# Graph aggregation with a sorted edge list: one allowance per tile for the second part's work, and evictions on VectorE after it

## The chip, the cores and the metric

The kernel runs on one core of a Trainium2 chip. The metric is the device time of one execution in microseconds (us). A core has engines that run side by side, each in its own order and waiting for the others by semaphores: TensorE (PE; its weight loads are PEld), VectorE (DVE), ScalarE (ACT), GpSimd (POOL) and SyncE (SP, which only issues DMAs here).

## What is computed

12,500 nodes have 64 features each; 800,000 edges have a source and a destination. For every node the features of its edges' sources are summed, scaled by a given number per node, and two 64 x 64 products are added:

```python
def reference(x, src, dst, deg_inv, w_self, w_neigh):
    N = x.shape[0]
    nsum = _segment_sum(x[src], dst, N)
    h_neigh = nsum * deg_inv[:, None]
    return x @ w_self + h_neigh @ w_neigh
```

The edges are random, so nothing is known of their order.

## The kernel before

Each edge becomes a 32-bit key: which block of 160 destinations and which block of 128 sources it joins (98 x 78 = 7644 such pairs, called buckets), and the places in both blocks. 128 partitions sort 6250 keys each; then the sorted runs are brought together. This is done in two parts: part 0 holds the first 4736 buckets, part 1 the rest. For each part, windows of the sorted runs are gathered by GpSimd to one row per partition (`gather_runs`), the row is merged (`merge_runs`, mostly minima and maxima on VectorE, L416 and L456), each bucket's start is searched (`find_and_gather`: a count, L616, on VectorE for part 1, then a gather, L620, on GpSimd), and the buckets are decoded (`decode_buckets`: `split` on VectorE, L657 to L662, `narrow` and `turn`, L667 to L678, casts on ScalarE and transposes on TensorE). A bucket has 128 slots; what doesn't fit is kept by its eight largest of each piece (`pieces`, L711) and put in order by `leftovers`. `tail` does the last few nodes, which no block of 160 holds. `check` sums counters to see that every edge is found.

The sums are the loop `nodes`: 962 tiles of eight buckets. VectorE makes two one-hots for 28 buckets at a time (`ohs` L838, `ohd` L841, together called a pair here), as far as 44 buckets ahead. TensorE multiplies one with the source features into a tile `ct` in PSUM (L867); an engine evicts it to `xg` (ScalarE L877, or VectorE L875); TensorE multiplies `xg` with the other one-hot into an accumulator (L923) that holds six blocks of destinations, 73.5 tiles. Leftover edges come in as gathered rows `lx` (GpSimd L887, five held at a time) with a mask `ohl` (VectorE L895) and two matmuls (L903). `finish` multiplies the sums by the weights and writes the output.

The order is the code's own here: every engine runs its instructions in the order in which the program writes them. While `nodes` goes on with part 0's buckets, the rest of part 1's work is written between its tiles, by `sums_and_merge`. There, n is the tile. From tile 8 on, PACE = 420 is added to t for each tile, and merge steps are written while t is above zero; each gives its cost in ns, which is taken off t. They stop after the first stages until tile 100 (RESUME). After the merge the search goes a step every second tile, then the decoding a step every tile, and then the leftovers; t plays no part in these. From tile 503 on (SHARE) every second tile is evicted by VectorE if enough one-hots are ready; the check is written at once behind the leftovers.

Of the kernel before, what the change touches and what calls it, by code (L numbers as in the profile page):

```python
# [11 lines left out]
F32 = mybir.dt.float32  # L12
# [21 lines left out]
KPRS = (37, 23)  # L34
# [24 lines left out]
PACE = 420  # L59
SHARE = 503  # L60
# [87 lines left out]
def on_act2(part, k):  # L148

    return part == 0 and (k < NLOWER or (k - NLOWER) % 2 == 0)  # L150
# [111 lines left out]
class Kernel:  # L262
# [381 lines left out]
    def decode_buckets(self, part, v, vp, mps):  # L644
# [51 lines left out]
        nc.vector.tensor_tensor(e, ext, bases(0, kpr, EXT), op=OP.bitwise_xor)  # L696
        f = e.bitcast(F32)
# [8 lines left out]
        yield kpr  # L706

    def pieces(self, f, n, top, pcs):

        for j in range(pcs):  # L710
            self.nc.vector.max(out=top[:, j, :8], in_=view(f, j, [[pcs, len(range(j, n, pcs))]]))  # L711

    def leftovers(self, part, mps):
# [6 lines left out]
        self.pieces(self.top.rearrange("p j i -> p (j i)"), PCS * 9, top.bitcast(F32), REST)  # L720
        k = top.rearrange("p j i -> p (j i)")
        yield 1
# [8 lines left out]
        yield 1  # L731
# [4 lines left out]
        nc.vector.scalar_tensor_tensor(q, t, float(HN), q, op0=OP.mult, op1=OP.add)  # L736
        nc.vector.tensor_scalar(t, k, 14, 1, op0=OP.logical_shift_right, op1=OP.bitwise_and)
# [3 lines left out]
        yield 1  # L741
# [18 lines left out]
    def tail(self, mps):  # L760
# [7 lines left out]
        yield  # L768
        yield
# [74 lines left out]
    def nodes(self, pool, aps, mps):  # L844
# [151 lines left out]
    def check(self, pool, mps):  # L996

        nc = self.nc
        self.flag = self.keep.tile([1, 1], I32, name="flag")
        ones = pool.tile([128, 1], F32, name="ones")  # L1000
        nc.vector.memset(ones, 1.0)
        one = pool.tile([128, 1], F32, name="one")
        nc.vector.tensor_reduce(one, self.cnt, axis=mybir.AxisListType.X, op=OP.add)
        ps = mps.tile([1, 1], F32, name="fps", tag="ct", bufs=3)
        nc.tensor.matmul(ps, one, ones, start=True, stop=True)
        nc.vector.tensor_scalar(self.flag, ps, float(E), None, op0=OP.not_equal)
# [119 lines left out]
    def sums_and_merge(self, es, mps, aps, u1, other, l2, l2b, l2a, va, vp):  # L1126
# [32 lines left out]
        self.picked, self.used = -9, 0  # L1159
        left, left_at = self.leftovers(0, mps), 2  # L1160
        t = 0
        for n in self.nodes(fin, aps, mps):
            if left and n >= left_at:
                wait = next(left, None)
                if wait is None:
                    left = None
                    if 1 in self.left:
                        self.check(fin, mps)
                else:
                    left_at = n + wait  # L1170
            if runs and n % 3 == 0:
                self.gather_runs(1, u1, [runs.pop(0)])
            if tail and n % 2:
                next(tail, None)
            if merge and n >= 8 and (n >= RESUME or steps < 2 * per):
                t += PACE
                while merge and t > 0:
                    dt = next(merge, None)
                    steps += 1
                    if dt is None:  # L1180
                        merge = None
                        self.merged = True
                        assert self.rows is u1
                        l2b.close()
                        vp = vb.enter_context(tc.tile_pool(name="vb", bufs=1))
                        self.windows(1, vp)
                        self.store_rows(2, tc.nc.scalar)
                        find = self.find_and_gather(1, range(KPRS[1]), LAG)
                    else:
                        t -= dt  # L1190
            elif find:
                if n % 2 == 0 and self.picked < n - 1 and next(find, None) is None:
                    find = None
                    decode = self.decode_buckets(1, self.v, vp, mps)
                    tail = self.tail(mps)
            elif decode:
                if next(decode, None) is None:
                    assert n < 128 * KPRS[0] // 8 - 12
                    decode = None
                    left, left_at = self.leftovers(1, mps), 0  # L1200
        vb.close()
# [28 lines left out]
```

## Time and profile before

| what | us |
|---|---|
| median of 3 runs | 1882.71 (1881.04 to 1889.39) |
| profiled execution | 1888.32 |
| its span, first to last instruction | 1886.6 |
| VectorE busy | 1667.2 |
| ScalarE busy | 1169.7 |
| TensorE busy with matmuls | 980.7 |
| GpSimd busy | 809.9 |

Busy times overlap, so they don't add up. A row of a table by stretches gives the stretch and its length, then for each engine its busy time and, in brackets, the number of instructions, then the granted TensorE clock as a share, the DMA's share and GB/s. A row of the timeline gives start, length, engine, line, operation, what is written and read, a count, and in square brackets how long the engine was idle before and what ended it. A row of waits gives who waited for whom: total, times, longest. A group's row gives the count, busy time, mean in ns, and idle time before with what ended most of it.

### The profile page before, as it was taken

The numbers are of one execution on the slowest core, as the hardware profiler recorded it, in microseconds if no ns is written. First come the engines' busy times: TensorE is split into PE (matmuls) and PEld (weight loads), VectorE is DVE, ScalarE is ACT, GpSimd is POOL, SyncE is SP. The second block draws the span as 40 slices with busy tenths as digits, with TensorE's granted clock in tenths as the row PEclk, the third lists the DMA queues.
The fourth block names the chain that finished last, engine by engine and source line by source line (L and its number), as shares of the span: only waits on it lengthen the run. The fifth ranks groups of instructions, "written<-read, shape, count | busy, mean of one in ns | idle before, by whom it ended". The sixth has DMA issues, their size and how long they took to land.

```text
span 1886.6 us, 54681 instructions
## 1 busy us (share of the span) xinstructions
PE 980.7 (52%) x23698; PEld 839.0 (44%) x23698; DVE 1667.2 (88%) x1805; ACT 1169.7 (62%) x1868; POOL 809.9 (43%) x917
## 2 busy tenths in 40 slices
PE   0015100000000000185888888888868989988997
PEld 0003100000000000174777777777757778777886
DVE  6999999999559999797799999998897888888885
ACT  7435128206500032485898888889977877877786
POOL 1000000798889986888713131313552142222321
PEclk9998655555555555598899999999999999999999
DMA  4304100011100012476678877779766888788784
GB/s 153 70 0 100 36 32 7 21 35 38 22 19 9 10 45 79 127 267 194 211 228 240 264 238 262 244 253 329 264 203 228 267 274 264 253 277 254 247 261 144
DMA packets 104805, 305.25 MB, mean 162 GB/s; under 512 B 52945, under 2 KB 60491, under 8 KB 103915
## 3 DMA queue, kind: packets, MB, share of 16 engines
q1 hardware_dynamic: 86347, 277.44, 41.7%
q0 software_dynamic: 17632, 22.17, 8.8%
q8 instruction: 187, 3.06, 0.6%
q10 hardware_dynamic: 576, 2.07, 0.3%
q14 instruction: 63, 0.52, 0.1%
HBM read 282.20 MB, written 19.41 MB: 160 GB/s over the span
## 4 chain that ended last, share of the span: by engine, by line
DVE 42%; PE 25%; POOL 13%; issue 10%; ACT 5%; DMA 4%; DVEq 0%; SPq 0%; ACTq 0%; POOLq 0%
DVE u L456 15%; PE ct L867 13%; POOL u L394 10%; PE acc L923 9%; DVE b L230 6%; DVE a L230 6%; DVE ohd L841 6%; DVE ohs L838 4%; DMA slb<-sl 2%; ACT xg L877 2%; POOL pad L307 2%; POOL lx L887 1%; DVE u L416 1%; PE acc L903 1%; POOL v L620 1%
## 5 line engine op out<-in xcount | busy, mean ns | idle before, releaser
L877 ACT ACTIVATE xg<-ct 128x1024 f16<-128x1024 f32 (+1 forms) x898 | 852.2, 1033 | 187.3 <-PE ct L867 154.8
L867 PE MATMUL ct<-xh,ohs 128*128 128x128 f16 x7644 | 545.4, 224 | 80.3 <-DVE ohs L838 40.0
L867 PEld LDWEIGHTS <-ohs 128*128 128x128 f16 x7644 | 450.2, 100 | 125.6 <-issue 64.2
L394 POOL DMA_INDIRECT u<-d,ix x256 | 374.0, 1461 | 178.8 <-DVE ix L386 135.4
L923 PE MATMUL acc<-ohd,xg 64*128 64x80 f16 x15288 | 405.9, 199 | 64.2 <-issue 48.9
L456 DVE TENSOR_TENSOR u<-u 128x1456 f32<-128x1456 f32 (+51 forms) x314 | 398.1, 1291 | 19.7 <-ACT u L421 13.6
L923 PEld LDWEIGHTS <-xg 64*128 64x128 f16 x15288 | 319.7, 96 | 135.0 <-issue 65.2
L841 DVE TENSOR_TENSOR ohd<-iota,dlT 128x2240 f16<-128x2240 bf16 x273 | 359.8, 1318 | 0.0
L838 DVE TENSOR_SCALAR ohs<-slb,pidx 128x3584 f16<-128x3584 bf16 x273 | 314.7, 1153 | 35.1 <-PE ct L867 16.6
L887 POOL DMA_INDIRECT lx<-xt,lsrc x140 | 231.2, 1652 | 261.6 <-PE acc L903 228.4
L230 DVE TENSOR_TENSOR b<-a 128x608 f32<-128x608 f32 (+44 forms) x124 | 173.8, 1444 | 6.3 <-ACT a L232 2.3
L230 DVE TENSOR_TENSOR a<-b 128x608 f32<-128x608 f32 (+44 forms) x124 | 173.9, 1445 | 4.5
L994 POOL DMA_DIRECT2D out<-o x25 | 23.7, 949 | 339.6 <-DVE o L993 257.6
L384 PE MATMUL stp<-idf,st 128*128 128x128 f32 x2 | 0.9, 445 | 310.7 <-DVE st L382 310.7
L677 PE MATMUL tr<-idb,l 128*128 128x128 bf16 x60 | 8.0, 273 | 263.9 <-ACT l L671 253.2
L384 PEld LDWEIGHTS stp<-idf,st 128*128 128x128 f32 x2 | 0.4, 183 | 311.1 <-issue 311.1
L875 DVE CAST xg<-ct 128x1024 f16<-128x1024 f32 x64 | 78.2, 1223 | 68.3 <-PE ct L867 63.5
L677 PEld LDWEIGHTS <-l 128*128 128x128 bf16 x60 | 4.9, 117 | 267.1 <-ACT l L671 255.7
L421 ACT ACTIVATE u<-u 128x96 f32<-128x96 f32 (+36 forms) x155 | 32.9, 258 | 134.3 <-DVE u L456 71.1
L375 ACT ACTIVATE junka<-b,c 128x132 bf16<-128x132 f32 (+46 forms) x205 | 90.8, 443 | 12.3 <-DVE b L230 5.8
L232 ACT ACTIVATE b<-a 128x1 f32<-128x1 f32 (+21 forms) x52 | 18.7, 379 | 128.1 <-DVE a L230 122.2
L620 POOL DMA_INDIRECT v<-d,ix x60 | 73.8, 1230 | 55.5 <-ACT ix L638 46.1
(160 smaller groups left out, 795.5 us busy)
## 6 DMA issues: line engine op xcount, KB each, us to landing
slb<-sl SPq DMA_DIRECT2D x273, 896.0 KB
u<-d,ix POOLq DMA_INDIRECT x256
xt<-xh SPq DMA_DIRECT2D x1, 3136.0 KB
fo<-own SPq DMA_DIRECT2D x26, 120.0 KB
own<-os SPq DMA_DIRECT2D x12, 256.0 KB
out<-o POOLq DMA_DIRECT2D x24, 120.0 KB
lx<-xt,lsrc POOLq DMA_INDIRECT x140
rd<-dst SPq DMA_DIRECT2D x4, 521.0 KB
```

What stands on the lines that cost most here:

```text
L230: nc.vector.tensor_tensor(view(dst, lo + sh, [[st, g], [1, l]]), x, y, op=op)
L375: nc.scalar.activation(junks[0][:, :n], w, AF.Sign, bias=self.c1[:, 0, c:c + 1], accum_out=a)
L394: nc.gpsimd.indirect_dma_start(out=u[:nr, EDGE + p * w:EDGE + (p + 1) * w], out_offset=None, in_=src, in_offset=bass.IndirectOffsetOnAxis( ...
L456: nc.vector.tensor_tensor(view(dst, EDGE + o + out, d), view(src, EDGE + o + x, d), view(src, EDGE + o + x + gap, d), op=op)
L620: self.nc.gpsimd.indirect_dma_start(out=self.v[:, k].bitcast(F32), out_offset=None, in_=flat(self.d2[home(part, k)], 128 * PITCH2[home(par ...
L838: nc.vector.tensor_scalar(s.rearrange("p c s -> p (c s)"), b, self.pidx[:, :1], None, op0=OP.is_equal)
L841: nc.vector.tensor_tensor(d, self.iota[:, None].to_broadcast([128, 14, HN, 2]), ix, op=OP.is_equal)
L867: nc.tensor.matmul(ct[:, i * 128:(i + 1) * 128], cols[i][0], self.xh[:, (b0 + i) % NB].rearrange("p a f -> p (a f)"), start=True, stop=True)
L875: nc.vector.tensor_copy(xg[:, :cnt * 128], ct[:, :cnt * 128])
L877: nc.scalar.activation(xg[:, :cnt * 128], ct[:, :cnt * 128], AF.Copy)
L887: nc.gpsimd.indirect_dma_start(out=x, out_offset=None, in_=self.xt, in_offset=bass.IndirectOffsetOnAxis(ap=self.left[p][1][:, c:c + 1], ax ...
L923: nc.tensor.matmul(acc[h][:, db % OCT * HN:(db % OCT + 1) * HN], xg[r, i * 128:(i + 1) * 128], d[r], start=db % OCT == 0 and sb == 0, stop ...
```

## The change

PACE becomes 390 and SHARE goes. t is added to at every tile from the eighth on, except in the pause before tile 100, also when the merge is over: a search step whose count is on VectorE takes 500 off it, and a decoding step is written only if t is above zero, begins five tiles after the search and takes off what it gives: 2300 if it holds a split, 0 if not, 1500, 800, 800, and 900 for each four maxima. So the exclusive or, the two products and the sixteen maxima, which were two steps, become seven. The leftovers of part 1 go a piece every second tile, in one or two pieces more, the tail's first work waits four turns more, and the check is three steps eight tiles apart, after the tail. VectorE evicts a tile only when `spare` is set, which is when part 1's leftovers are done.

```diff
-PACE = 420
-SHARE = 503
+PACE = 390
...
-            yield min(step // 2 * 4, kpr - 1)
+            yield 2300 if step % per == 0 and step // per < len(groups) else 0
...
         nc.vector.tensor_tensor(e, ext, bases(0, kpr, EXT), op=OP.bitwise_xor)
+        yield 1500
...
-        yield kpr
+            yield 800
...
-        self.pieces(f.rearrange("p k h s -> p (k h s)"), kpr * 2 * EXT, top, PCS)
+        for _ in self.pieces(f.rearrange("p k h s -> p (k h s)"), kpr * 2 * EXT, top, PCS, 4):
+            yield 900
...
             self.nc.vector.max(out=top[:, j, :8], in_=view(f, j, [[pcs, len(range(j, n, pcs))]]))
+            if j % per == per - 1:
+                yield
...
-            pend.append(gather(b0, cnt, t >= SHARE))
+            pend.append(gather(b0, cnt, self.spare))
...
         nc.vector.tensor_reduce(one, self.cnt, axis=mybir.AxisListType.X, op=OP.add)
+        yield
         ps = mps.tile([1, 1], F32, name="fps", tag="ct", bufs=3)
         nc.tensor.matmul(ps, one, ones, start=True, stop=True)
+        yield
...
                 if wait is None:
                     left = None
                     if 1 in self.left:
-                        self.check(fin, mps)
+                        self.spare = True
...
-            if tail and n % 2:
-                next(tail, None)
-            if merge and n >= 8 and (n >= RESUME or steps < 2 * per):
-                t += PACE
-                while merge and t > 0:
+            if tail and n % 2 and next(tail, self) is self:
+                tail = None
+            if self.spare and not tail and n % 8 == 0 and verdict != self:
+                verdict = verdict or self.check(fin, mps)
+                if next(verdict, self) is self:
+                    verdict = self
+            if n < 8 or (merge and n < RESUME and steps >= 2 * per):
+                continue
+            t += PACE
+            while merge and t > 0:
...
+            if find and n % 2 == 0 and self.picked < n - 1:
+                k = next(find, None)
+                if k is None:
                     find = None
-                    decode = self.decode_buckets(1, self.v, vp, mps)
                     tail = self.tail(mps)
-            elif decode:
-                if next(decode, None) is None:
+                elif k < KPRS[1] and not on_act2(1, k):
+                    t -= 500
+            if not find:
+                ready += 1
+            if decode and ready > 4 and t > 0:
+                dt = next(decode, None)
+                if dt is None:
...
+                else:
+                    t -= dt
```

Lines from L687 on move by a few (L838 becomes L842, L875 L879, L456 L455). Counted along each engine's order, the merge's end stands behind 410 evictions before and 434 now, the last search step behind 481 and 505, the casts of part 1's buckets between 488 and 510 and between 515 and 538 evictions by ScalarE, and the first eviction by VectorE at about tile 504 and 566; there are 64 of these before and 55 now.

VectorE near the merge's end, before: a merge stage (`u<-u`) stands between any two pairs of one-hots.

```order
L456 TENSOR_TENSOR u<-u 128x1456
L838 TENSOR_SCALAR ohs<-slb,pidx 128x3584
L841 TENSOR_TENSOR ohd<-iota,dlT 128x2240
L456 TENSOR_TENSOR u<-u 128x1456
L838 TENSOR_SCALAR ohs<-slb,pidx 128x3584
L841 TENSOR_TENSOR ohd<-iota,dlT 128x2240
L456 TENSOR_TENSOR u<-u 128x1456
L838 TENSOR_SCALAR ohs<-slb,pidx 128x3584
L841 TENSOR_TENSOR ohd<-iota,dlT 128x2240
```

And now, at the same place:

```order
L455 TENSOR_TENSOR u<-u 128x1456
L842 TENSOR_SCALAR ohs<-slb,pidx 128x3584
L845 TENSOR_TENSOR ohd<-iota,dlT 128x2240
L899 TENSOR_SCALAR ohl<-wide,lp_2834 128x160
L842 TENSOR_SCALAR ohs<-slb,pidx 128x3584
L845 TENSOR_TENSOR ohd<-iota,dlT 128x2240
L455 TENSOR_TENSOR u<-u 128x1456
L842 TENSOR_SCALAR ohs<-slb,pidx 128x3584
L845 TENSOR_TENSOR ohd<-iota,dlT 128x2240
```

Now and then two pairs, 56 buckets, stand between two merge stages.

VectorE where the last buckets of part 1 are decoded, before (`u` is the exclusive or and its products, `top` and `ltop` the maxima, `lz` the start of the leftovers):

```order
L875 CAST xg<-ct 128x1024
L696 TENSOR_TENSOR u<-v,c_1_68 128x1426
L699 SCALAR_TENSOR_TENSOR u<-u,v 128x23x31 x2
L838 TENSOR_SCALAR ohs<-slb,pidx 128x3584
L841 TENSOR_TENSOR ohd<-iota,dlT 128x2240
L703 MEMSET top_18093 128x144
L711 MAX top_18093<-u 128x8 x16
L711 MAX ltop<-top_18093 128x8 x8
L838 TENSOR_SCALAR ohs<-slb,pidx 128x3584
L841 TENSOR_TENSOR ohd<-iota,dlT 128x2240
L725 TENSOR_SCALAR lz,cnt<-ltop 128x64
```

And now:

```order
L695 TENSOR_TENSOR u<-v,c_1_68 128x1426
L699 SCALAR_TENSOR_TENSOR u<-u,v 128x23x31
L842 TENSOR_SCALAR ohs<-slb,pidx 128x3584
L845 TENSOR_TENSOR ohd<-iota,dlT 128x2240
L699 SCALAR_TENSOR_TENSOR u<-u,v 128x23x31
L703 MEMSET top_18968 128x144
L711 MAX top_18968<-u 128x8 x12
L842 TENSOR_SCALAR ohs<-slb,pidx 128x3584
L845 TENSOR_TENSOR ohd<-iota,dlT 128x2240
L711 MAX top_18968<-u 128x8 x4
L711 MAX ltop<-top_18968 128x8 x4
L842 TENSOR_SCALAR ohs<-slb,pidx 128x3584
```

The two products and the maxima have pairs of one-hots between them, and no eviction (`xg<-ct`) stands among them.

GpSimd at the end of the tail's gathers (`tx`), before:

```order
L669 DMA sl<-l_17945 128x384
L788 DMA tx<-xt,ts 128x128
L887 DMA lx<-xt,lsrc_2825 128x128
L788 DMA tx<-xt,ts 128x128 x4
L887 DMA lx<-xt,lsrc_2825 128x128 x2
L994 DMA out<-o 120x4x64
L887 DMA lx<-xt,lsrc_2825 128x128
```

And now:

```order
L668 DMA sl<-l_18726 128x384
L792 DMA tx<-xt,ts 128x128 x2
L891 DMA lx<-xt,lsrc_2836 128x128
L792 DMA tx<-xt,ts 128x128 x5
L998 DMA out<-o 120x4x64
L891 DMA lx<-xt,lsrc_2836 128x128
L792 DMA tx<-xt,ts 128x128
L891 DMA lx<-xt,lsrc_2836 128x128 x4
```

The tail's gathers stand a place later among the leftovers' (`lx`) and the outputs, with at most five of them in a row.

More of the change, by code (lines that the diff above doesn't have):

```diff
@@ L719, in leftovers @@
         top = pool.tile([128, REST, 8], I32, name="ltop")
-        self.pieces(self.top.rearrange("p j i -> p (j i)"), PCS * 9, top.bitcast(F32), REST)
+        for _ in self.pieces(self.top.rearrange("p j i -> p (j i)"), PCS * 9, top.bitcast(F32), REST, 4):
+            yield 1 + part
         k = top.rearrange("p j i -> p (j i)")
-        yield 1
         t = pool.tile([128, n], I32, name="lt")
@@ L730, in leftovers @@
         nc.vector.tensor_tensor(s, s, t, op=OP.bitwise_or)
-        yield 1
+        yield 1 + part
         q = pool.tile([128, n], I32, name="lq")
@@ L736, in leftovers @@
         nc.vector.scalar_tensor_tensor(q, t, float(HN), q, op0=OP.mult, op1=OP.add)
+        if part:
+            yield 2
         nc.vector.tensor_scalar(t, k, 14, 1, op0=OP.logical_shift_right, op1=OP.bitwise_and)
@@ L740, in leftovers @@
         nc.vector.tensor_tensor(z, z, q, op=OP.add)
-        yield 1
+        yield 1 + part
         sel = pool.tile([128, 64], F32, name="sel")
@@ L767, in tail @@
         nc.gpsimd.dma_start(k.bitcast(F32), last.rearrange("(p n) -> p n", n=n))
-        yield
-        yield
+        for _ in range(6):
+            yield
         t = pool.tile([128, n], I32, name="tt")
@@ new lines, in sums_and_merge @@
+            if self.spare and not tail and n % 8 == 0 and verdict != self:
[6 more added lines that the diff above has]
+            while merge and t > 0:
+                dt = next(merge, None)
+                steps += 1
+                if dt is None:
+                    merge = None
+                    self.merged = True
+                    assert self.rows is u1
+                    l2b.close()
+                    vp = vb.enter_context(tc.tile_pool(name="vb", bufs=1))
+                    self.windows(1, vp)
+                    self.store_rows(2, tc.nc.scalar)
+                    find = self.find_and_gather(1, range(KPRS[1]), LAG)
+                    decode = self.decode_buckets(1, self.v, vp, mps)
+                    ready = 0
+                else:
+                    t -= dt
@@ L1200, in sums_and_merge @@
                     left, left_at = self.leftovers(1, mps), 0
+                else:
+                    t -= dt
+        assert verdict is self
         vb.close()
```

26 lines of the change are left out of this document (8 added, 18 removed).

## The prediction

> **What bounds the kernel now.** I read the page first (busy times, costliest groups), then the table of stretches, the same table for tile `xg` alone, which counts the evictions and so the tiles, then the waits and the timeline where a tile takes long.
>
> ```profile
> PE 980.7 (52%) x23698; PEld 839.0 (44%) x23698; DVE 1667.2 (88%) x1805; ACT 1169.7 (62%) x1868; POOL 809.9 (43%) x917
> ...
> L877 ACT ACTIVATE xg<-ct 128x1024 f16<-128x1024 f32 (+1 forms) x898 | 852.2, 1033 | 187.3 <-PE ct L867 154.8
> L875 DVE CAST xg<-ct 128x1024 f16<-128x1024 f32 x64 | 78.2, 1223 | 68.3 <-PE ct L867 63.5
> ```
>
> VectorE is the busiest over the span. The second part, the loop over 962 tiles, runs from 799 us to the end; by stretches (PE, PEld, DVE, ACT, POOL busy us):
>
> ```profile
> 799.00:930.00 131.00, 102.24 (x2434) 87.77 (x2433) 106.75 (x133) 98.96 (x135) 114.11 (x149) 0.89 0.70 235
> 930.00:1273.00 343.00, 290.91 (x7528) 253.21 (x7525) 339.97 (x319) 300.01 (x357) 87.10 (x48) 0.99 0.76 243
> 1273.00:1356.00 83.00, 74.68 (x1854) 63.65 (x1849) 73.72 (x112) 75.85 (x104) 41.32 (x34) 0.98 0.91 312
> 1356.00:1388.00 32.00, 24.29 (x584) 20.15 (x585) 27.93 (x53) 30.90 (x42) 21.98 (x19) 1.00 0.68 212
> 1388.00:1426.00 38.00, 27.09 (x598) 23.05 (x590) 31.96 (x81) 20.72 (x28) 9.12 (x8) 0.87 0.46 157
> 1426.00:1468.00 42.00, 36.15 (x924) 31.58 (x922) 34.39 (x38) 30.84 (x34) 12.98 (x10) 0.96 0.84 275
> 1468.00:1876.00 408.00, 371.53 (x9520) 325.24 (x9517) 336.51 (x364) 326.85 (x358) 116.46 (x78) 0.97 0.80 254
> ```
>
> The evictions in them (here PE, PEld, DVE, ACT; the last two counts are the evictions):
>
> ```profile
> 799.00:930.00 131.00, 44.98 (x1592) 34.92 (x1592) 0.00 (x0) 94.68 (x101) 0.89 0.70 235
> 930.00:1273.00 343.00, 126.47 (x4928) 100.74 (x4928) 0.00 (x0) 291.26 (x310) 0.99 0.76 243
> 1273.00:1356.00 83.00, 32.91 (x1214) 25.52 (x1208) 0.00 (x0) 73.17 (x77) 0.98 0.91 312
> 1356.00:1388.00 32.00, 9.36 (x365) 7.39 (x366) 1.34 (x2) 22.98 (x24) 1.00 0.68 212
> 1388.00:1426.00 38.00, 11.71 (x374) 8.70 (x366) 4.75 (x4) 18.52 (x21) 0.87 0.46 157
> 1426.00:1468.00 42.00, 15.89 (x608) 12.76 (x608) 6.10 (x5) 30.56 (x32) 0.96 0.84 275
> 1468.00:1876.00 408.00, 163.80 (x6200) 129.14 (x6200) 66.06 (x54) 319.52 (x338) 0.97 0.80 254
> ```
>
> Dividing gives us per tile: 1.106 while the second part's runs are merged (930 to 1273, VectorE busy 99%), 1.078 in the search, 1.231 in the bucket casts (1356 to 1388, ScalarE 97%), 1.520 in 1388 to 1426, 1.135 to 1468, and 1.041 for the last 392 tiles, where no engine is above 91%. So three things cost more than the last stretch's pace: VectorE in the merge, ScalarE in the casts, and something in 1388 to 1468. That last is the worst, and the timeline names it:
>
> ```profile
> 1387.87 1.22 DVE L875 CAST xg<-ct 128x1024 f16<-128x1024 f32 x1 [0.30 <-PE ct L867]
> 1389.01 1.63 DVE L696 TENSOR_TENSOR u<-v,c 128x1426 int32<-128x1426 int32 x1
> 1390.68 1.72 DVE L699 SCALAR_TENSOR_TENSOR u<-u,v 128x713 f32<-128x713 int32 x2
> 1394.88 3.47 DVE L711 MAX8 top<-u 128x8 f32<-128x90 f32 x16
> 1404.26 1.22 DVE L875 CAST xg<-ct 128x1024 f16<-128x1024 f32 x1
> 1416.01 0.15 DVE L1006 TENSOR_SCALAR flag<-fps 1x1 int32<-1x1 f32 x1 [0.37 <-PE fps L1005]
> ...
> 1399.37 0.19 PE L923 MATMUL acc<-ohd,xg 64*128 64x80 f16 x1 [0.52 <-issue]
> 1405.53 1.25 PE L923 MATMUL acc<-ohd,xg 64*128 64x80 f16 x32 [3.48 <-DVE xg L875]
> 1415.78 0.19 PE L1005 MATMUL fps<-ones,one 128*1 128x1 f32 x2 [3.59 <-DVE one L1003]
> ```
>
> VectorE has no idle row from 1387.87 to 1415.6. TensorE stands 3.48 us for an eviction that is queued on VectorE behind the maxima and the leftovers' arithmetic, and 3.59 us for the check's sum, queued the same way.
>
> **The change, part by part.** The instructions are the same but for nine evictions (55 on VectorE for 64). What moves is where they stand.
>
> *Smaller pace, merge.* The order has the merge's end behind 434 tiles instead of 410. The merge's own work is unchanged; the stretch takes in 24 more tiles, and as VectorE is its bound each adds what VectorE does for a tile, the one-hots:
>
> ```profile
> 1484.78 1.15 DVE L838 TENSOR_SCALAR ohs<-slb,pidx 128x3584 f16<-128x3584 bf16 x1
> 1485.84 1.32 DVE L841 TENSOR_TENSOR ohd<-iota,dlT 128x2240 f16<-128x2240 bf16 x1
> 1487.07 1.15 DVE L838 TENSOR_SCALAR ohs<-slb,pidx 128x3584 f16<-128x3584 bf16 x1
> ...
> 1425.86 3.77 ACT L877 ACTIVATE xg<-ct 128x1024 f16<-128x1024 f32 x4 [0.22 <-PE ct L867]
> ```
>
> From one pair to the next are 2.29 us for 28 buckets, 3.5 tiles: 0.654 us a tile, 15.7 us for 24. The same 24 tiles leave the end of the loop, where they take 24 x 1.041 = 25.0. The term is -9.3 us. The merge then runs at (343 + 15.7) / 334 = 1.074 us a tile, still above 1.041, so VectorE stays its bound, though barely, and TensorE's own waits begin to show:
>
> ```profile
> PE ct L867 <- DVE ohs L838: 21.4, 24, 1.8
> PE acc L923 <- issue: 14.7, 12, 2.7
> ```
>
> The 21.4 us that TensorE waits for one-hots in 930 to 1273 is more than the 9.3 that I take out of it, so the gain is there to be had; but the 14.7 us of its issue waits are hidden behind a late VectorE now and would be less so. I take -8, with 0 and -9.3 as ends.
>
> *Before tile 100.* The first merge steps end six to seven tiles later. L456's own busy time in the merge is
>
> ```profile
> 930.00:1273.00 343.00, 124.63 (x84) 0.99 0.76 243
> ```
>
> for 310 tiles, 0.40 a tile; six tiles are 2.4 us. VectorE is idle 24 of 131 us in 799 to 930, which covers it; if that cover fails, +2.4. I take 0.
>
> *Search and allowance.* The search still goes a step per two tiles and takes 500 for a count while it earns 780, so some 9,500 ns of credit are there when the bucket work begins. That spends 6 x 2300 = 13,800 in 24 tiles that earn 9,360, so the credit never runs out: the casts come four tiles apart as before, and the allowance divides nothing there. Search and casts cost what they did, 1.078 and 1.231 a tile; the four tiles' pause between them costs nothing, as it holds only evictions. The casts lose their two VectorE evictions to a ScalarE that is 97% busy: by the row of four in a chain, 0.94 each, +1.9 us. The other seven go where ScalarE is busy 20.72 of 38 us: 0; without that cover they would be +6.6.
>
> *Long steps divided, evictions later, check in steps.* 1388 to 1468 is 80 us for 62 tiles, 15.5 above the last stretch's pace. VectorE's 27.7 us from 1387.87 are five one-hot pairs (11.5), three evictions (3.4 at a pitch of 1.13, from the rows 1387.87 and 1389.01) and 12.8 of second-part work. Up to the last of the tail's masks that work stands among four pairs now: 12.8 + 9.2 + 3.4 = 25.4 us of VectorE for 14 tiles, which at 1.041 would take 14.6, so VectorE falls 10.8 behind. In the new order it stands among five pairs, without an eviction: 12.8 + 11.5 + 1.6 for leftover masks and an output = 25.9 us for 17.5 tiles, 18.2 at 1.041, 7.7 behind. Three pairs with almost nothing between follow, so that it catches up. One-hots run 44 buckets, 5.5 tiles, ahead; that takes up some of the 7.7 in both orders. The largest piece between two pairs is half the products and twelve maxima, 0.9 + 12/16 of 3.47 = 3.5 us. So the work is only a little thinner; what really goes is that TensorE and ScalarE wait for an eviction or a sum behind it (3.48 and 3.59). I leave in 4 us of VectorE's 7.7 and 3.3 of issue waits of some 0.5 us around 1390 to 1400 (about seven). Term: -(15.5 - 4 - 3.3), taken as -8. Ends: -15.5, if nothing of it stays, and -2, if the waits come back elsewhere. Late next would be TensorE itself. The check's matmul now stands eight tiles behind its sum, some 8 us; nothing of TensorE is behind a wait there. GpSimd's fourteen tail gathers and six stores meet leftover gathers and outputs as before, and the tail begins four turns later; POOL is busy 21.98 of 32 us in the casts, so 0.
>
> Sum: -8 + 0 + 1.9 - 8 = -14.1 us. The profiled execution took 1888.32 (span 1886.6 and 1.7 around it), 5.6 above the median of the three runs; 1888.3 - 14.1 = 1874.2 there, 1868.6 from the median 1882.71. I say 1868.
>
> **The rivals.** *The pace gives nothing.* TensorE's issue waits take the place of its waits for one-hots and the merge stays at 1.106. For it: 1.074 is only 3% above 1.041. Against: in 930 to 1273 ScalarE and TensorE are at 87% and 85%. Then -8 + 1.9, or down to -2 + 1.9 if the dense stretch pays little too: 1877 to 1883, no change that can be told.
>
> *A gather is late (slower).* TensorE has stood for a leftover's rows once:
>
> ```profile
> 888.92 0.45 PE L903 MATMUL acc<-ohl,lx 128*128 128x160 f16 x2 [14.88 <-DMA lx<-xt,lsrc]
> ```
>
> GpSimd had a queue of gathers ahead of it. The 101 tiles of 799 to 930 take 131 us, at the merge's 1.106 they would take 112: 19 us for one such wait with what follows. Now the group that ends at tile 515 meets stores that wait for the casts and then the tail's gathers. One such wait leaves 1868 + 19 = 1887, no change; from the second on it decides, 1906. Against: five rows are held ahead, used three tiles apart at the closest, 15 tiles or 16 us; and the most that the new order puts between two of these gathers is five of the tail's:
>
> ```profile
> 1391.77 1.81 POOL L788 DMA_INDIRECT tx<-xt,ts  x1 [0.30 <-issue]
> 1395.81 0.94 POOL L788 DMA_INDIRECT tx<-xt,ts  x1 [0.30 <-issue]
> ```
>
> At 1.81 + 0.3 each, 10.6 us, under 16. That the two rows differ bears on it: 1391.77 runs beside two-input work and a one-hot, 1395.81 beside maxima. The Trainium skill, page "SBUF — State Buffer", section "SBUF: two separate sides", says that VectorE in a two-port mode locks GpSimd out of a shared port, so that descriptors of a GpSimd DMA are not written until it ends. It speaks against this change: fewer evictions from PSUM and more one-hots per us on VectorE would make every gather slower; by it the five would still be priced by the longer of the rows, and the 0.9 us difference agrees with it without showing the cause. By that rule alone the sum is unchanged and this rival's chance is 0.10 instead of the 0.05 that I would give by the 10.6 us.
>
> *More than forecast.* All of 15.5 and 9.3 less 1.9 are 22.9 us, 1860; with a last stretch that is quicker too, 1857 or less. Nothing in the profile speaks for the latter.
>
> **How the numbers follow.** A change of 0.5% is 9.4 us here, about what this measurement tells from none: below 1873.3 is faster, above 1892.1 slower. Forecast (1857 to 1873): 0.57. More: 0.06. Pace gives nothing or the dense stretch keeps its waits (1873 to 1883): 0.22. One late gather (about 1887): 0.05; two or more: 0.10. Faster 0.63, same 0.27, slower 0.10. For 8 in 10 the range goes from 1856, which leaves out most of the high gains, to 1885, which leaves out the late gathers; the forecast's own is 1857 to 1873.
>
> **What would show it.** In the profile after: tiles 100 to 434 at about 1.07 us with VectorE still at 97% or more, and TensorE's waits for one-hots there about halved; the 26 tiles of casts still 1.2 or more; no TensorE wait over 3 us on VectorE behind tile 504, and 1.0 to 1.2 us a tile from the casts to the first VectorE eviction at about tile 566; the last stretch at 1.04. Wrong if the merge stays at 1.10, if a wait for `lx` appears near tile 515, or if the last stretch is slower.

## The result and the profile after

The changed kernel takes 1859.07 us, the median of four runs (1854.63 to 1865.24), against 1882.64 for the kernel before beside it: a ratio of 0.9873, 95% interval 0.9847 to 0.9899, so 23.6 us less. In two later sets, each on another chip, the same file gave 0.9960 (0.9932 to 0.9989) and 0.9918 (0.9890 to 0.9947); the table of the experiments has them. The mean of the three ratios is 0.9917, the forecast's was 1868 / 1882.71 = 0.9922. The intervals of the first two don't overlap, so how much the change is worth differs from set to set by more than the scatter within a set.

The profiled execution took 1865.24, its span 1863.4. Its busy times:

```profile
PE 981.3 (53%) x23698; PEld 843.6 (45%) x23698; DVE 1657.2 (89%) x1796; ACT 1174.9 (63%) x1877; POOL 806.9 (43%) x917
```

VectorE does 10 us less, nine evictions. The second part by stretches: to tile 100, merge, search, casts, the decoding and tail, the rest.

```profile
799.00:925.00 126.00, 100.00 (x2447) 86.59 (x2446) 108.48 (x134) 98.86 (x135) 109.66 (x146) 0.90 0.73 246
925.00:1288.00 363.00, 318.59 (x8112) 277.88 (x8109) 358.04 (x339) 321.14 (x381) 95.45 (x54) 0.96 0.78 251
1288.00:1369.00 81.00, 72.83 (x1829) 62.99 (x1822) 70.73 (x109) 75.43 (x104) 46.23 (x35) 0.98 0.91 311
1369.00:1408.00 39.00, 31.65 (x743) 27.03 (x743) 35.57 (x60) 37.62 (x51) 18.40 (x17) 0.96 0.70 231
1408.00:1442.00 34.00, 31.29 (x799) 27.42 (x796) 33.65 (x82) 29.77 (x37) 17.52 (x14) 0.95 0.79 247
1442.00:1852.00 410.00, 366.80 (x9540) 321.80 (x9538) 336.82 (x368) 327.24 (x357) 113.75 (x80) 0.98 0.79 254
```

The same table for tile `xg` alone, whose last two counts are the evictions:

```profile
925.00:1288.00 363.00, 138.29 (x5312) 110.98 (x5312) 0.00 (x0) 313.94 (x334) 0.96 0.78 251
1369.00:1408.00 39.00, 13.08 (x472) 10.14 (x471) 0.00 (x0) 28.92 (x30) 0.96 0.70 231
1408.00:1442.00 34.00, 13.13 (x512) 10.61 (x512) 1.22 (x1) 29.13 (x32) 0.95 0.79 247
1442.00:1852.00 410.00, 161.50 (x6216) 127.58 (x6216) 66.03 (x54) 320.14 (x337) 0.98 0.79 254
```

So the merge runs at 363 / 334 = 1.087 us a tile with VectorE busy 99%, the casts at 1.30 with ScalarE 96%, what was the worst stretch at 1.03 for 33 tiles, and the last at 1.049. To see what belongs to the change, here is the time between the ends of evictions, worked out from the traces, in three profiles of the changed kernel. The tiles of a row are those of the new order; of before the same work is taken, which in the row of the merge is 310 tiles and in the row below the search 85 tiles.

| stretch (us) | before | after | 2nd profile | 3rd profile |
|---|---|---|---|---|
| tiles 0 to 100 | 130.5 | 123.8 | 131.5 | 131.5 |
| merge (310; 334 after) | 343.8 | 363.5 | 358.4 | 358.0 |
| search (75) | 82.1 | 80.6 | 81.6 | 83.8 |
| casts, decoding, tail (85; 61 after) | 112.7 | 72.8 | 81.7 | 86.0 |
| tiles 570 to 961 | 408.4 | 410.4 | 410.1 | 405.7 |
| sum | 1077.5 | 1051.1 | 1063.3 | 1065.0 |

The 24 tiles that move are worth 25.0 us at the last stretch's pace. The merge therefore gained 25.0 - 19.7 = 5.3, 10.4 and 10.8 us in the three profiles, and the casts to tail gained 112.7 - 25.0 less what they take now: 14.9, 6.0 and 1.7. The first profile is the luckiest in two rows, to tile 100 and in the casts to tail, and both are those in which GpSimd issues many gathers. The mean of the three gains in the casts to tail, 7.5 us, is near the 6.1 of the forecast, but no profile shows that figure as a steady one.

In 925 to 1288 what TensorE waits for (`issue` is idle time that no semaphore in the profile explains):

```profile
PE ct L871 <- DVE ohs L842: 15.0, 20, 1.8
PE acc L927 <- issue: 14.9, 10, 3.4
```

The same two rows for 930 to 1288 in the second profile, then in the third:

```profile
PE ct L871 <- DVE ohs L842: 11.7, 16, 1.7
PE acc L927 <- issue: 13.3, 12, 2.1
...
PE ct L871 <- DVE ohs L842: 12.9, 18, 1.8
PE acc L927 <- issue: 12.1, 10, 3.7
```

And every wait of TensorE over 1 us from 1360 to 1442 in the timeline:

```profile
1365.26 0.34 PE L871 MATMUL ct<-xh,ohs 128*128 128x128 f16 x3 [1.49 <-issue]
1371.20 0.24 PE L927 MATMUL acc<-ohd,xg 64*128 64x80 f16 x3 [1.57 <-issue]
1382.31 0.19 PE L927 MATMUL acc<-ohd,xg 64*128 64x80 f16 x1 [1.74 <-ACT g L932]
1431.30 1.03 PE L871 MATMUL ct<-xh,ohs 128*128 128x128 f16 x8 [2.58 <-DVE ohs L842]
```

The 3.48 us for an eviction and the 3.59 us for the check's sum are gone; one wait for one-hots of 2.58 us is left. In the second and third profiles no TensorE wait for VectorE reaches 1 us between the casts and tile 570.

### The profile page after: what moved, and what is told of

The parts are those of the page before. It is cut to its first block, busy times and chain, and to the rows that moved or that the text cites. A ratio compares the mean times of both kernels' runs of the same rounds, so it can differ in the third digit from the quotient of the medians.

```text
span 1863.4 us, 54695 instructions
## 1 busy us (share of the span) xinstructions
PE 981.3 (53%) x23698; PEld 843.6 (45%) x23698; DVE 1657.2 (89%) x1796; ACT 1174.9 (63%) x1877; POOL 806.9 (43%) x917
## 4 chain that ended last, share of the span: by engine, by line
DVE 37%; PE 31%; POOL 13%; issue 11%; ACT 5%; DMA 3%; DVEq 0%; SPq 0%; ACTq 0%; POOLq 0%
PE ct L871 16%; DVE u L455 13%; PE acc L927 12%; POOL u L393 10%; DVE a L229 6%; DVE b L229 6%; DVE ohd L845 4%; DVE ohs L842 3%; ACT xg L881 2%; POOL pad L306 2%; PE po L990 1%; POOL lx L891 1%; DMA slb<-sl 1%; DVE u L415 1%; PE pw L598 1%
## 5 line engine op out<-in xcount | busy, mean ns | idle before, releaser
L881 ACT ACTIVATE xg<-ct 128x1024 f16<-128x1024 f32 x907 | 860.5, 1047 | 157.9 <-PE ct L871 137.9
L393 POOL DMA_INDIRECT u<-d,ix x256 | 367.5, 1435 | 174.9 <-DVE ix L385 131.3
L927 PE MATMUL acc<-ohd,xg 64*128 64x80 f16 x15288 | 401.5, 199 | 58.9 <-issue 41.2
L455 DVE TENSOR_TENSOR u<-u 128x1456 f32<-128x1456 f32 (+51 forms) x314 | 397.6, 1290 | 9.2 <-ACT u L420 3.3
L842 DVE TENSOR_SCALAR ohs<-slb,pidx 128x3584 f16<-128x3584 bf16 x273 | 314.7, 1153 | 37.9 <-PE ct L871 31.0
L879 DVE CAST xg<-ct 128x1024 f16<-128x1024 f32 x55 | 67.3, 1223 | 59.2 <-PE ct L871 58.9
L231 ACT ACTIVATE b<-a 128x1 f32<-128x1 f32 (+21 forms) x52 | 18.8, 381 | 128.7 <-DVE a L229 122.9
```

Of the source, the lines that this page charges most:

```text
L393: nc.gpsimd.indirect_dma_start(out=u[:nr, EDGE + p * w:EDGE + (p + 1) * w], out_offset=None, in_=src, in_offset=bass.IndirectOffsetOnAxis( ...
L455: nc.vector.tensor_tensor(view(dst, EDGE + o + out, d), view(src, EDGE + o + x, d), view(src, EDGE + o + x + gap, d), op=op)
L842: nc.vector.tensor_scalar(s.rearrange("p c s -> p (c s)"), b, self.pidx[:, :1], None, op0=OP.is_equal)
L879: nc.vector.tensor_copy(xg[:, :cnt * 128], ct[:, :cnt * 128])
L881: nc.scalar.activation(xg[:, :cnt * 128], ct[:, :cnt * 128], AF.Copy)
L927: nc.tensor.matmul(acc[h][:, db % OCT * HN:(db % OCT + 1) * HN], xg[r, i * 128:(i + 1) * 128], d[r], start=db % OCT == 0 and sb == 0, stop ...
```

## The experiments

Twelve runs in three sets of four, each set on another chip with the kernel before beside it. A ratio is to the kernel before of the same set.

| run | us | ratio (95%) | before, same set |
|---|---|---|---|
| e1, pace alone | 1877.95 | 0.9955 (0.9927 to 0.9983) | 1888.19 |
| e2, all but the pace | 1877.72 | 0.9924 (0.9890 to 0.9958) | 1888.19 |
| e3, evictions from tile 503 | 1879.61 | 0.9942 (0.9904 to 0.9980) | 1888.19 |
| e4, whole steps | 1879.05 | 0.9946 (0.9910 to 0.9983) | 1888.19 |
| e5, changed kernel, 2nd | 1880.05 | 0.9960 (0.9932 to 0.9989) | 1887.79 |
| e6, check at once | 1876.27 | 0.9935 (0.9908 to 0.9962) | 1887.79 |
| e7, pace 360 | 1875.81 | 0.9952 (0.9922 to 0.9982) | 1887.79 |
| e8, no evictions on VectorE | 1866.70 | 0.9881 (0.9841 to 0.9921) | 1887.79 |
| e9, changed kernel, 3rd | 1879.50 | 0.9918 (0.9890 to 0.9947) | 1895.49 |
| e10, before, no evictions on VectorE | 1867.85 | 0.9855 (0.9827 to 0.9883) | 1895.49 |
| e11, none, and pace 360 | 1867.84 | 0.9851 (0.9820 to 0.9882) | 1895.49 |
| e12, tail's gathers plain | 1868.38 | 0.9885 (0.9849 to 0.9921) | 1895.49 |

### The pace alone, and all but the pace

The kernel before with one number changed:

```diff
-PACE = 420
+PACE = 390
```

> The kernel before with the smaller pace (390) and nothing else; evictions on VectorE still from tile 503, long steps whole, check at once. Theory A (each part gives its own share; between the two profiles the stretch from tile 100 to the merge's end took 343.8 us for 310 tiles before and 363.5 us for 334 after, so 24 tiles cost 19.7 instead of 25.0 at the end of the loop): 5 us under before, 1878. Rival B (the pace is what gave most, by way of an emptier queue in all that follows): 15 us or more under before, 1868 or less. Rival C (without the other parts a later merge brings search and casts under the evictions of VectorE from tile 503 on and loses): 1883 or more.

The changed kernel with that number put back:

```diff
-PACE = 390
+PACE = 420
```

> The kernel after with the pace put back to 420: divided steps, late evictions and the check in steps alone. Theory A: what the profiles show behind the merge, 28.2 us above 1.041 us a tile before and 11.8 after, so 16 us under before, 1866. Rival B: 1875 or more.

Each half is faster than before by itself, 0.45% and 0.76%, and the intervals overlap: which half is worth more is not told. The pace alone came out at the 1878 of theory A. The rest alone gave 10.5 us where theory A had 16, and its 1877.72 lies where rival B had put it. The two ratios multiply to 0.988, which the first comparison reached and the two later ones did not. The profile of the pace alone has this row for the merge, and with 336 evictions in it, 1.065 us a tile:

```profile
930.00:1288.00 358.00, 317.76 (x8133) 277.89 (x8127) 356.97 (x337) 321.56 (x383) 100.13 (x50) 0.97 0.81 253
```

VectorE is busy 99.7% of it. The forecast said 1.074, so the mechanism of the pace is as it was told: VectorE bounds the merge, and tiles put among it cost less than at the end.

The row of the casts, the decoding and the tail, worked out as in the table above, took 85.4 us for 61 tiles with the pace alone, 2.3 less than the kernel before would give (112.7 - 25.0 = 87.7), and TensorE stood there for VectorE's evictions, 6.73 us once. With the rest alone it took 98.3 for 85 tiles, 14.4 less. So in these two profiles it is the rest that shortens this stretch, but two profiles of the whole change, with 6.0 and 1.7, show far less.

### One part of the rest undone

Evictions on VectorE from tile 503, as before:

```diff
-            pend.append(gather(b0, cnt, self.spare))
+            pend.append(gather(b0, cnt, t >= 503))
```

> The kernel after with VectorE's evictions from tile 503 again, all else kept. Theory A (an eviction queued on VectorE behind second-part work makes TensorE and ScalarE wait, and ScalarE alone can do these tiles): 5 to 8 us over the kernel after, 1865 to 1867, with waits of TensorE for VectorE's evictions of 2 us and more between tiles 510 and 566. Rival D (the divided steps keep such waits short, and the casts gain from evictions that ScalarE need not make): 1859 or less.

Decoding's steps and the leftovers whole again:

```diff
-        yield 1500
...
-            yield 800
+        yield 3100
...
         for _ in self.pieces(f.rearrange("p k h s -> p (k h s)"), kpr * 2 * EXT, top, PCS, 4):
-            yield 900
+            pass
+        yield 3600
...
         for _ in self.pieces(self.top.rearrange("p j i -> p (j i)"), PCS * 9, top.bitcast(F32), REST, 4):
-            yield 1 + part
+            pass
+        yield 1
...
-        yield 1 + part
+        yield 1
...
-        if part:
-            yield 2
```

> The kernel after with the long steps whole again (exclusive or and products in one step, sixteen maxima in one, the leftovers' pieces as before a tile apart); pace, late evictions and the check in steps kept. Theory A (the work is only a little thinner when it is divided, five pairs of one-hots for four): 1 to 3 us over the kernel after, 1860 to 1862. Rival E (the division is what gave the gain): 8 us or more over it, 1867 or more.

The check run in one go where `spare` is set:

```diff
                     if 1 in self.left:
                         self.spare = True
+                        for _ in self.check(fin, mps):
+                            pass
+                        verdict = self
```

> The kernel after with the check written whole in one turn as soon as part 1's leftovers are done. Theory A (TensorE waited 3.59 us for the sum before, as VectorE was late; where VectorE is not late the wait is the 0.4 us of the sum itself): same as the kernel after, within 2 us. Rival G (the wait returns and halves the clock behind it): 5 us over it.

The ratios are 0.9942, 0.9946 and 0.9935; the changed kernel's own in two sets are 0.9960 and 0.9918. No changed kernel ran in the first set, so the two of that set are compared with it across sets only. None of the three parts, undone alone, costs what a measurement can tell. With evictions from tile 503 the waits that theory A names are back, 2.93 and 3.55 us at tiles 528 and 556, though its 5 to 8 us can't be told:

```profile
1393.12 0.47 PE L927 MATMUL acc<-ohd,xg 64*128 64x80 f16 x16 [2.93 <-DVE xg L879]
...
1432.44 0.71 PE L927 MATMUL acc<-ohd,xg 64*128 64x80 f16 x16 [3.55 <-DVE xg L879]
```

With whole steps the row of the casts to the tail took 75.1 us, close to the shortest of the changed kernel, so the divided steps are not seen to shorten it. With the check at once TensorE does not stand 1 us for its sum. The Trainium skill, page "Perfetto Trace Analysis", section "Optimizing Scalar/DVE Operations", says that breaking up instructions of an engine that isn't saturated but makes others wait may let work finish sooner. Here, with the instructions kept and the steps broken up between tiles, no gain of that can be told: the ratio with whole steps, 0.9946, lies between the changed kernel's own 0.9960 and 0.9918.

### A smaller pace still

```diff
-PACE = 390
+PACE = 360
```

> The kernel after with a pace of 360: the merge ends some 27 tiles later again. Theory A (24 tiles cost 19.7 instead of 25.0 us at the last step, and the merge then nears the 1.041 us a tile of the last stretch): 2 to 4 us under the kernel after. Rival H (the merge stretch is bound by TensorE by now, and search, casts and leftovers come together with the end of part 0): same or over it.

1875.81 against 1880.05, intervals overlapping: no further gain that can be told, and no loss.

### The changed kernel again

The same file in the second and the third set.

> The kernel after, unchanged, beside the next three. Theory A (pace and the rest add up, e1 gave 0.45% and e2 0.76%): 0.988 of before. Rival F (the first comparison was lucky; each part and the whole give the same half per cent): 0.993 or more.

> The kernel after once more, beside the next three. What is open is its size: 0.9873 in the first comparison, 0.996 in e5. Theory M (the first profile had none of the stretches in which TensorE starts four to ten matmuls and then stands 0.3 to 0.5 us, the one of e5 had 14 us of them; the gain is some 15 us less where they come): 0.990 to 0.996, with such stretches in the profile. Rival N (the difference is the chip's alone): 0.987 or 0.996, without a relation to them.

1880.05 and 1879.50 us, 7.7 and 16.0 less than before. The second ratio, 0.9960, is on the side of rival F; the third, 0.9918, came with the stops in its profile, as theory M has it. The third profile shows what the first did not have. Its rows for the merge, for 34 evictions after the casts, and for the rest:

```profile
930.00:1288.00 358.00, 318.26 (x8118) 277.59 (x8118) 355.92 (x337) 321.48 (x384) 96.87 (x51) 0.97 0.79 252
1411.00:1460.00 49.00, 39.69 (x802) 33.19 (x798) 34.26 (x82) 30.87 (x38) 14.52 (x14) 0.79 0.58 170
1460.00:1866.00 406.00, 366.87 (x9564) 320.44 (x9558) 337.22 (x369) 327.64 (x358) 117.18 (x80) 0.99 0.80 257
```

The merge is fast here, 1.07 a tile. But 1411 to 1460 takes 1.44 a tile with the clock granted at 0.79, where the first profile took 34.00 us for 33 evictions at 0.95. No engine is busy throughout: the busiest, TensorE, has 39.69 of 49. TensorE's timeline in it:

```profile
1410.33 0.76 PE L927 MATMUL acc<-ohd,xg 64*128 64x80 f16 x32
...
1413.12 0.26 PE L927 MATMUL acc<-ohd,xg 64*128 64x80 f16 x4 [0.39 <-issue]
1413.85 0.31 PE L927 MATMUL acc<-ohd,xg 64*128 64x80 f16 x5 [0.48 <-issue]
1414.63 0.26 PE L927 MATMUL acc<-ohd,xg 64*128 64x80 f16 x4 [0.47 <-issue]
...
1421.14 0.69 PE L871 MATMUL ct<-xh,ohs 128*128 128x128 f16 x5 [0.81 <-issue]
1421.76 1.25 PE L927 MATMUL acc<-ohd,xg 64*128 64x80 f16 x32
```

From 1413 to 1421 it does a few matmuls and stops, mostly every 0.74 us, with no semaphore to wait for, and afterwards the same 32 matmuls take 1.25 us instead of 0.76. GpSimd in that time:

```profile
1412.57 0.95 POOL L891 DMA_INDIRECT lx<-xt,lsrc  x1 [0.30 <-issue]
1413.82 0.95 POOL L792 DMA_INDIRECT tx<-xt,ts  x1 [0.30 <-issue]
...
1418.82 0.94 POOL L792 DMA_INDIRECT tx<-xt,ts  x1 [0.30 <-issue]
```

Six gathers, one each 1.25 us. The traffic of the DMA queues (packets, MB, share) in 1400 to 1410 and in 1410 to 1420, of this profile:

```profile
q1 hardware_dynamic: 370, 2.42, 67.3%
q0 software_dynamic: 224, 0.39, 15.9%
q8 instruction: 2, 0.03, 1.2%
...
q1 hardware_dynamic: 177, 1.05, 30.6%
q0 software_dynamic: 303, 0.36, 16.1%
```

The queue that brings instructions, q8, starts two packets in the first stretch and none in the second; the next one starts at 1420.0 and lands at 1421.0, and the stops end. In the first profile of the changed kernel the same queue starts two in its 1410 to 1420, and there are no stops, though GpSimd issues gathers in a row there too. So the reading is that TensorE runs out of instructions when a packet comes late, and that gathers in a row have to do with it. The other direction isn't excluded: VectorE stands idle for 5.09 us while TensorE stops, and GpSimd's gathers are quickest when VectorE is idle.

Counted as three or more stops of 0.25 to 0.6 us that follow one another within 1.5 us, over the second part such stops are (length of the stretches, idle time in them) 10.8 and 7.2 us in the profile of before, none in the first of the changed kernel, 14.2 and 8.6 in the second, 10.4 and 6.4 in the third. In these they lie where GpSimd issues one gather behind another, near 895 us and between 1325 and 1435. The places are mostly the same in all fourteen profiles: tile 72 (near 895 us) in every one but the first of the changed kernel, which is also the only one that takes less than 128 us for tiles 0 to 100; and tiles 539 to 542, or tile 570 at a pace of 360, again among the tail's gathers, in seven of the ten that have the new order and these gathers. So the first profile, the one of the first comparison, was a lucky one.

### The tail's gathers taken out

```diff
-            nc.gpsimd.indirect_dma_start(
-                out=rows[:, c], out_offset=None, in_=self.xt,
-                in_offset=bass.IndirectOffsetOnAxis(ap=s[:, c:c + 1].bitcast(U32), axis=0))
+            nc.sync.dma_start(rows[:, c], self.xt[c * 128:(c + 1) * 128])
```

> The kernel after with the tail's fourteen gathers by GpSimd replaced by plain copies of fixed rows on SyncE's queue (so the last nodes' rows are not the right ones). Theory M (TensorE's stop and go comes while GpSimd issues gathers one after the other): no such stretch between tiles 509 and 570, and 5 to 10 us under e9 where e9 has them. Rival O (they come from something else there): the same stretches, within 3 us of e9.

1868.38 us, 11.1 less than the changed kernel of the same set, though the two intervals overlap. The stretch, with 33 evictions in it:

```profile
1414.00:1447.00 33.00, 30.49 (x806) 26.74 (x800) 32.72 (x81) 30.06 (x37) 8.00 (x6) 1.00 0.74 237
```

33 us at the full clock, 1.00 a tile, for the 1.44 of the third profile, and no stops in tiles 509 to 570. It is one profile, three of the ten with the gathers in place have no stops there either, and the first one of the changed kernel reached 1.03. The run agrees with the gathers as cause but doesn't show it; that they act by holding up instruction packets is read from the coincidence above and was not shown apart.

### No evictions on VectorE

The changed kernel, and the kernel before, with all 962 evictions on ScalarE:

```diff
-            pend.append(gather(b0, cnt, self.spare))
+            pend.append(gather(b0, cnt, False))
```

> The kernel after with every eviction on ScalarE, none on VectorE. Theory A (in the last stretch no engine is above 91% and TensorE sets the pace; 55 evictions more make ScalarE 0.94 x 393 = 370 us busy of 410): 0 to 5 us over the kernel after. Rival I (an eviction on VectorE stands in the way of one-hots and costs more than it saves): 3 us or more under it.

```diff
-SHARE = 503
+SHARE = 9999
```

> The kernel before with all evictions on ScalarE and nothing else changed. Theory J (an eviction on VectorE costs more than it saves, also in the last stretch: 397.3 us for tiles 570 to 961 in e8, 410 in the kernel after and 408 before): 12 us from the last stretch and some 4 from the one ahead of it, 0.990 to 0.993 of before. Rival K (e8 gained by what it has besides): 0.996 or more.

1866.70, 13.4 less than the changed kernel in its set, and 1867.85, 11.7 less than it in the other; in both sets the intervals are apart. Rival I and theory J have the direction right; the old kernel gained 27.6 us, more than theory J's 16. One number in the old kernel is worth more in its set than the whole change. The last 391 evictions take (no evictions on VectorE, from the changed kernel):

```profile
1454.00:1851.00 397.00, 368.16 (x9548) 321.02 (x9540) 279.73 (x314) 369.85 (x411) 104.71 (x80) 0.99 0.81 261
```

and in the kernel before without them:

```profile
1463.00:1853.00 390.00, 368.04 (x9528) 321.09 (x9527) 278.69 (x309) 369.00 (x411) 103.69 (x78) 0.99 0.82 266
```

408 to 390 is 18 us, between two single profiles. All fourteen profiles can be compared from tile 610 on, where part 1's work is over in each of them: the eleven with evictions on VectorE take 363.1 to 377.4 us to the last tile, the three without 351.7, 357.0 and 360.4. ScalarE, which takes over 54 evictions, is busy 369 of 390 and isn't the bound yet. The waits of the last stretch in the kernel before, who waits for whom, in us, times and longest:

```profile
ACT xg L877 <- PE ct L867: 75.3, 92, 3.5
DVE xg L875 <- PE ct L867: 58.6, 40, 3.9
...
PE acc L923 <- issue: 22.7, 22, 2.8
...
PE ct L867 <- issue: 8.7, 8, 2.5
```

and without the evictions on VectorE:

```profile
DVE ohs L838 <- PE ct L867: 99.5, 87, 3.0
...
ACT xg L877 <- PE ct L867: 19.1, 37, 2.3
...
PE acc L923 <- issue: 8.8, 12, 1.9
...
PE ct L867 <- issue: 3.8, 6, 1.9
```

Before, VectorE stands 58.6 us in front of evictions whose tile TensorE has not made yet, and the one-hots behind them stand too; without them its waiting, 99.5, is for room to run ahead. But TensorE hardly stood for VectorE before either: 0.6 us for its evictions in this stretch and nothing for one-hots. What TensorE gets back is in its two issue rows: 31.4 us before, 12.6 without, 18.8 less for the 18 us. All but 1.2 of the 31.4 ends 1.1 to 1.7 us after a packet of q8 has landed. Why an eviction on VectorE leaves TensorE more such waits is not shown by these runs.

### None of them, and the pace at 360

```diff
-PACE = 390
+PACE = 360
...
-            pend.append(gather(b0, cnt, self.spare))
+            pend.append(gather(b0, cnt, False))
```

> The kernel after with every eviction on ScalarE and a pace of 360. Theory J with what e7 gave (0.9952 for 0.996): as e8 or 1 to 3 us under it, 0.987. Rival H (ScalarE alone makes the longer merge dearer): 0.990 or more.

1867.84, the same as the kernel before without these evictions, 1867.85, and 0.9851 is on theory J's side. So neither the change nor a smaller pace adds anything that can be told to leaving all evictions on ScalarE, and the plain version with `SHARE = 9999` is the simplest of the versions that beat both kernels in their sets.

## Why the prediction was right, step by step

**The time.** 1859.07 lies in the range of 1856 to 1885 on the side of faster, 9 us below the 1868; the two repeats, at 0.9960 and 0.9918, stand for 1875.2 and 1867.3 from a before of 1882.71. The forecast's size is that of the three together; the first result was the best of them, from a set whose profile was free of stops, and 1875.2 would have been in the 1873 to 1883 that the prediction kept for its rivals. That a single comparison falls this clearly to the side of faster is partly luck.

**Smaller pace, -8.** Right: 5.3, 10.4 and 10.8 us in three profiles, and faster by 0.45% with this alone. The two larger lie 1 to 1.5 us past the end given, -9.3. The merge took 358.4 / 334 = 1.073 us a tile in the second profile and 1.072 in the third, where 1.074 was said; in the first it took 1.088. TensorE's waits for one-hots fell from 21.4 to 15.0, 11.7 and 12.9, between a third and nearly the half that was said; its issue waits were 14.9, 13.3 and 12.1 for 14.7, so the fear that they would grow in the place of the others did not come true. The rival that the pace gives nothing falls.

**Before tile 100, 0.** Right for the change: 131.5 in two profiles, 1 us more than before. The first profile's 123.8 is 6.7 less; what goes with it is something that the prediction didn't have, the missing stops of TensorE near 895 us. The prediction read that 19 us loss as one late gather; the wait itself is still there in all three profiles, 14 to 16 us:

```profile
890.61 0.45 PE L907 MATMUL acc<-ohl,lx 128*128 128x160 f16 x2 [15.78 <-DMA lx<-xt,lsrc]
```

**Search and allowance.** Search unchanged, 80.6 to 83.8 for 82.1: right. The casts stay bound by ScalarE at 96%, 1.2 or more a tile (1.30, and 39 us for 32 evictions in the third profile): right.

**Casts lose two evictions, +1.9, and the dense work, -8: together -6.1.** Here the sizes failed. The three profiles give -14.9, -6.0 and -1.7. The step is "I leave in 4 us of VectorE's 7.7 and 3.3 of issue waits". What it names is right: VectorE still makes TensorE wait, once in the first profile (2.58 us), and the waits behind evictions and the check are gone. But the issue waits are not a fixed 3.3: they are none in the first profile, and in the third, with the slower matmuls that follow them, most of what 1411 to 1460 takes beyond the first profile's pace. The prediction saw seven of them in one profile and took their size for a fixed one; they keep to a few places but differ from run to run, and this term alone moves by 13 us. That, with the 7 us of the first row, is more than all of the 12 to 14 us by which the first profile's sum is below the other two; the merge goes the other way. The prediction's own sign, 1.0 to 1.2 us a tile from the casts to about tile 566, holds in the first profile only: tiles 538 to 565 took 1.09, 1.46 and 1.62.

**The late gather (slower).** Not seen: behind tile 100 no TensorE wait for `lx` in any of the three profiles. The Trainium skill's rule on the shared port (page "SBUF — State Buffer", section "SBUF: two separate sides"), which gave this rival its 0.10, has its row in this case, as the next section but one shows, and still no gather came late.

**The last stretch, 1.04 and unchanged.** Right as a forecast (1.04 to 1.05), and the place where most was to be had. The prediction took these 392 tiles as the pace to which all else was compared and did not ask what 54 evictions on VectorE cost there. Nine fewer of them, elsewhere, was in its sum as a loss of 1.9; all of them fewer was a gain of 12 to 13 us over the changed kernel.

What stays open: why the change is worth 1.3% in one set and 0.4% in another, and how much of the dense work's gain comes from which of its parts. The stops are one thing that differs between profiles, but no run counts how often they come in each set.

## What to carry to other kernels

Before a stretch with unexplained stops is priced from one profile, look at the same stretch in other places of that profile, or in other profiles: a loss that comes and goes can be larger than the change. Where work is shared between two engines that run in order, try giving all of it to one, even at 95% busy, before tuning when the sharing begins. It gained here, though TensorE was hardly seen to wait for the engine that helped, so the reason is left open. And a wait of TensorE for nothing that the profile names is worth setting beside the instruction queue's packets.

## What was not expected of the hardware

The traces suggest that TensorE can be short of instructions. The instruction queue q8 lands packets of 16 KB, 183 in the second part, about one each 5.8 us or five and a half tiles, and of the longer issue waits of TensorE (0.6 us or more, 32 to 66 us in all per profile) 464 of 500 in the fourteen profiles end 1.2 to 1.6 us after such a packet has landed. By chance it would be about one in twelve, an estimate from these two figures. That is a coincidence in the traces, found in every profile of this study, and not an experiment.

In the third profile the stops go with two losses: the ten issue waits from 1413 to 1421 add up to 5.3 us, and behind them 32 matmuls take 1.25 us for 0.76; the granted clock of 1411 to 1460 is 0.79.

GpSimd's indirect gathers take 0.94 to 0.98 us in all 13 cases of the third profile (930 to 1866 us) in which VectorE stands idle beside them, and 1.71 in the mean in the 35 that run beside `ohs` and `ohd` alone; 2.24 in the 20 with a merge step beside these. The 33 that run beside no `ohd` take 0.96 in the mean, 1.16 at most. The Trainium skill, page "SBUF — State Buffer", section "SBUF: two separate sides", says that GpSimd and VectorE share a port pair that one of them holds at a time, VectorE in a two-port mode, or with two inputs against a GpSimd operation that reads. The numbers agree with it, without showing the port, as far as `ohd` goes, which has two inputs; two-input work doesn't always do it, since a gather that ran beside one of the products (1412.57 in the third profile, shown above) took 0.95:

```profile
1412.61 0.90 DVE L699 SCALAR_TENSOR_TENSOR u<-u,v 128x713 f32<-128x713 int32 x1
```
